# One TensorE operation instead of two for each second-layer step of a fused attention and feed-forward kernel

## The chip, the cores and the metric

The kernel runs on one core of a Trainium2 chip. The metric is the device time in microseconds of one execution: three runs of the kernel before gave 417.93, 418.27 and 418.51, the median is 418.27 us. One further execution was taken with the hardware profiler; all rows of the trace come from that one.

Engines are named as the profile names them: PE is TensorE's matmul, PEld its load of the stationary operand, DVE is VectorE, ACT is ScalarE, POOL is GpSimd and SP is SyncE, which issues the DMAs.

## The reference

The reference has two halves. The first is attention over 4 batches, 8 heads, 768 positions and 64 features: each position sees its neighbours within a window of 16 and one summary for each block of 32 positions (maximum of the keys, mean of the values). The second takes the heads together as a 512-wide x and applies a gated feed-forward block with a hidden width of 1024:

```python
xk = mu_k * x + (1.0 - mu_k) * x_prev
xr = mu_r * x + (1.0 - mu_r) * x_prev
k = np.maximum(xk @ w_k, 0.0)
v = k * k @ w_v
r = 1.0 / (1.0 + np.exp(-(xr @ w_r)))
return r * v
```

x_prev is x one position earlier. The change is in `k * k @ w_v`, the second layer.

## The kernel before

**How precision is kept.** Most products are made with numbers split in two: a high part in TensorE's rounded 32-bit format and a low part that holds the rest. A product a @ w is then three products that add up in one bank: high a with high w, high a with low w, low a with high w.

**The halves.** Each batch is worked in two halves of 384 positions (`hf`), three tiles of 128. For every half but the two of the last batch there is: attention for four pairs of heads; the mixing of x and x_prev and its split; the gate (`gate_tile`, lines 717 to 719, 12 products of 512 columns to a tile); and `experts` (from line 740), the two layers. The last batch has its own path (`last_batch` and `seven`, lines 893 to 1050; its products stand at lines 929 and 1020), with no second-layer step of the kind that is changed.

**The two layers.** `experts` goes through the hidden width in eight tiles j of 128. `first(j)` makes 12 products of 384 columns into one bank (line 757, "e1"), then relu (ACT, line 764) and square (ACT, line 766). The square r is split: its high part kh is a copy on DVE (line 770) or on ACT (line 771), whichever the schedule chooses, and its low part kl is r minus kh, on DVE (line 772). `second(j)` (products at line 784, "e2") adds this tile's share to three result banks `acc`, one for each tile of positions. The step is split in two operations: e2a does for each bank the products of kh with the high and low weights, six in all, and waits for kh; e2b does for each bank the product of kl with the high weights, three in all, and waits for kl. The last step, j = 7, is three operations, one to a bank, each with its two products of kh and one of kl; DVE multiplies each finished bank by the gate (line 814), and SP stores it.

In the very first half the first five tiles (`PLAIN`) use unsplit numbers ("single"): four products for e1 and three for e2, slower ones, with no kl. The order of emission is first(0), first(1), second(0), first(2), second(1), and so on.

**Banks.** PSUM has eight banks. Four, the pool `mm`, serve the two layers and the gate: during a half three hold `acc` and one is left for e1. The other four serve attention; from batch 1 on they are one pool, `at`, of which a score operation takes four and a values operation two (lines 550, 358 to 364).

**What sets the order.** No order is written by hand. Each operation is told to a planner (`Plan`, line 133) with its engine, its length in ns from the table `LENGTH` (line 40), a due time, and what it reads and writes. `schedule` (line 171) first carries due times backwards: an operation must be done in time for those that read its result. Then it plays through the whole kernel, and gives each engine in turn the ready operation that can start earliest, by due time where several can start at once (line 237). Engines work off their lists strictly in this order on the chip; waits are semaphores. A changed length, due time or dependency may therefore change the order of everything that follows in the plan, on each engine and in SP's DMA queue too. Attention for a batch (score, line 559, masks at 585, exponentials at 589, normalisation on POOL at 601, transposes on DVE at 626, values at 656) is placed by this planner among the products of the batch before it.

Of the kernel before, what the change touches and what calls it, by code (L numbers as in the profile page):

```python
# [32 lines left out]
NTT = HT // P  # L33
# [5 lines left out]

LENGTH = dict(  # L40
    score=950, values2=1715, score2=1600, transpose=350, vturn=110, vpool=800, vsel=330, spread=540, spread_p=900, values=1020, gate=2740, gate32=930, e1=2100,
    e1_32=2690, e2a=1400, e2b=705, e2=705, e2_32=2600, e2l_32=930,
    warm=223, kred=865, kred2=470, kmax=90, kcopy=280, vred=865, mask=204, rc=320, evac=470, mixd=535, sub=475, khv=280,
    result=600, wbits=340, wor=610, wsub=605, tiny=60,
    exp=380, pts=375, vm=160, mixa=515, cast=405, relu=380, square=425, sigmoid=500, sigmoid3=1600, wscale=570, wcast=530,
# [87 lines left out]
class Plan:  # L133
# [4 lines left out]
    def buf(self, pool, dtype=F32, in_turn=True):  # L138
        n = self.count[pool] if in_turn else None
        self.count[pool] += in_turn  # L140
        self.unplaced[pool] += 1
        return Buf(pool, n, dtype)

    def op(self, eng, cost, due, emit, reads=(), writes=(), size=0, other=None):

        bufs = []
        for x, _ in list(reads) + list(writes):
            if isinstance(x, Buf) and x not in bufs:
                bufs.append(x)
        ways = {eng: (LENGTH.get(cost, 0), emit)}  # L150
        if other:
            ways[other[0]] = (LENGTH[other[1]], other[2])
        o = Op(len(self.ops), ways, due, bufs, size)
        for x in reads:
            o.deps.update(self.writers.get(x, ()))
        for x in writes:
            o.deps.update(self.writers.get(x, ()))
            o.deps.update(self.readers.get(x, ()))
        for x in reads:
            self.readers.setdefault(x, []).append(o)  # L160
        for x in writes:
            self.writers[x] = [o]
            self.readers[x] = []
        o.deps.discard(o)
        for x in bufs:
            x.users.append(o)
        self.ops.append(o)
        o.name = cost
        return o
# [139 lines left out]
def tile_kernel(ctx: ExitStack, tc: tile.TileContext, q, k, vT, v, consts, w_k, w_v, w_r, out):  # L309
# [7 lines left out]
    def slots(name, n, shape):  # L317
        return [Slot(const, f"{name}{i}", shape) for i in range(n)]
# [13 lines left out]
        kh=slots("kh", 2, [P, HT]), kl=slots("kl", 2, [P, HT]),  # L332
# [37 lines left out]
    op, buf = plan.op, plan.buf  # L370
# [21 lines left out]
    def e1_due(b, hf, j):  # L392
        if b + hf == 0:
            return GATE0 + 11000 + STEP0 * j
        return gate_due(b, hf) + 8400 + STEP * j

    def e2_due(b, hf, j):
        return e1_due(b, hf, j + 1) + 2200

    w_f, w_h, w_l = {}, {}, {}  # L400
# [339 lines left out]
    def experts(b, hf, x, z):  # L740

        plain = PLAIN if b + hf == 0 else (0, 0)
        tiles_of = [(j + (max(PLAIN) if (b, hf) == (0, 1) else 0)) % NCV for j in range(NCV)]
        acc, ks = [], {}

        def first(j):
            ps, r = buf("mm"), buf("r")
            single = j < plain[0]
            kh, kl = ks[j] = (r, None) if j < plain[1] else (buf("kh", F32R), buf("kl", F32R))
            h, l = (w_f["wk", tiles_of[j]], None) if single else (w_h["wk", tiles_of[j]], w_l["wk", tiles_of[j]])  # L750
            terms = [(h, 0)] if single else [(h, -2), (h, -1), (l, -2)]

            def products():
                n = 0
                for w, s in terms:
                    for p in range(NPAIR):
                        nc.tensor.matmul(ps.t[:, 0:HT], w.t[:, p * P:(p + 1) * P], x[p][s].t,  # L757
                                         start=(n == 0), stop=(n == len(terms) * NPAIR - 1))
                        n += 1

            op("PE", "e1_32" if single else "e1", e1_due(b, hf, j), products,
               reads=list(dict.fromkeys([(pair[s], 0) for pair in x for _, s in terms] + [(w, 0) for w, _ in terms])),
               writes=[(ps, 0)])
            op("ACT", "relu", None, lambda: nc.scalar.activation(r.t, ps.t[:, 0:HT], AF.Relu),  # L764
               reads=[(ps, 0)], writes=[(r, 0)])
            op("ACT", "square", None, lambda: nc.scalar.activation(r.t, r.t, AF.Square),  # L766
               reads=[(r, 0)], writes=[(r, 0)])
            if kl is None:
                return
            op("DVE", "khv", None, lambda: nc.vector.tensor_copy(out=kh.t, in_=r.t),  # L770
               reads=[(r, 0)], writes=[(kh, 0)], other=("ACT", "cast", lambda: nc.scalar.copy(out=kh.t, in_=r.t)))  # L771
            op("DVE", "sub", None, lambda: nc.vector.tensor_tensor(  # L772
                out=kl.t, in0=r.t, in1=kh.t.bitcast(F32), op=ALU.subtract),
               reads=[(r, 0), (kh, 0)], writes=[(kl, 0)])

        def second(j):
            kh, kl = ks[j]
            single = kl is None
            due = e2_due(b, hf, j)
            w = [(w_f["wv", tiles_of[j]], 0)] if single else [(d["wv", tiles_of[j]], 0) for d in (w_h, w_l)]  # L780

            def product(t, a, w, start=False, stop=False):
                v = w["wv", tiles_of[j]].t
                nc.tensor.matmul(acc[t].t, a.t[:, t * P:(t + 1) * P], v.bitcast(F32) if single else v, start=start, stop=stop)  # L784

            if j < NCV - 1:
                def high():
                    for t in range(NTT):
                        if single:
                            product(t, kh, w_f, start=(j == 0))  # L790
                        else:
                            product(t, kh, w_h, start=(j == 0))
                            product(t, kh, w_l)

                def low():
                    for t in range(NTT):
                        product(t, kl, w_h)

                op("PE", "e2_32" if single else "e2a", due, high, reads=[(kh, 0), *w], writes=[(a, 0) for a in acc])
                if not single:  # L800
                    op("PE", "e2b", due + 1400, low, reads=[(kl, 0), *w], writes=[(a, 0) for a in acc])
                return
            for t in range(NTT):
                def last(t=t):
                    if single:
                        product(t, kh, w_f, stop=True)
                    else:
                        product(t, kh, w_h)
                        product(t, kh, w_l)
                        product(t, kl, w_h, stop=True)  # L810

                op("PE", "e2l_32" if single else "e2", due + 700 * t, last,
                   reads=[(kh, 0), *([] if single else [(kl, 0)]), *w], writes=[(acc[t], 0)])
                op("DVE", "result", due + 4000 + 700 * t, lambda t=t: nc.vector.tensor_tensor(
                    out=z[t].t, in0=acc[t].t, in1=z[t].t, op=ALU.mult),
                   reads=[(acc[t], 0), (z[t], 0)], writes=[(z[t], 0)])
                row = hf * HT + t * P
                op("SP", "store", due + 5000 + 700 * t, lambda t=t, row=row: nc.sync.dma_start(
                    out=out[b, row:row + P, :], in_=z[t].t), reads=[(z[t], 0)], size=P * 2048)

        first(0)
        for j in range(1, NCV + 1):
            if j < NCV:
                first(j)
            if j == 1:
                acc.extend(buf("mm") for _ in range(NTT))
            second(j - 1)
# [375 lines left out]
```

## Time and profile before

| | |
|---|---|
| median of three runs | 418.27 us (417.93 to 418.51) |
| profiled execution, its own time | 418.56 us |
| its span, first to last instruction | 416.5 us |
| granted TensorE clock | 1.00 |
| DMA traffic | 79.68 MB, mean 191 GB/s |

A row of a window view gives the stretch, its length, then for each engine the busy time and number of instructions. In a row of groups stands: line, engine, operation, written and read tiles, sizes and count, then busy time, mean ns of one, and the idle time before them with what ended it. In the chain of waits a row is start, duration, engine and line; in a timeline it is start, duration, engine, line, operation and tiles, and in brackets the idle time before. A matmul's row is longer than its share of TensorE, because one is drained while the next runs; the distance from one start to the next is what it costs.

### The profile page before, as it was taken

The numbers are of one execution on the slowest core, as the hardware profiler recorded it, in microseconds if no ns is written. First come the engines' busy times: TensorE is split into PE (matmuls) and PEld (weight loads), VectorE is DVE, ScalarE is ACT, GpSimd is POOL, SyncE is SP. The second block draws the span as 40 slices with busy tenths as digits, with TensorE's granted clock in tenths as the row PEclk, the third lists the DMA queues.
The fourth block names the chain that finished last, engine by engine and source line by source line (L and its number), as shares of the span: only waits on it lengthen the run. The fifth ranks groups of instructions, "written<-read, shape, count | busy, mean of one in ns | idle before, by whom it ended". The sixth has DMA issues, their size and how long they took to land.

```text
span 416.5 us, 9788 instructions
## 1 busy us (share of the span) xinstructions
PE 409.1 (98%) x3353; PEld 348.1 (84%) x3353; DVE 344.8 (83%) x1053; ACT 286.8 (69%) x815; POOL 125.9 (30%) x255
## 2 busy tenths in 40 slices
PE   8899999999999999999999999999999999999996
PEld 7654557788888888988888888988889899999996
DVE  3889999999998799889798778569386698878993
ACT  2889999899874599547674559466595675669710
POOL 0472565534660043502252000422433030104100
PEclk9999999999999999999999999999999999999999
DMA  8996679678878577777635454487855325230012
GB/s 295 407 296 216 222 257 318 235 251 235 240 210 264 173 248 196 230 267 247 215 120 159 158 183 172 133 297 200 252 150 143 103 75 146 59 113 15 0 59 94
DMA packets 48193, 79.68 MB, mean 191 GB/s; under 512 B 6736, under 2 KB 28176, under 8 KB 48144
## 3 DMA queue, kind: packets, MB, share of 16 engines
q1 hardware_dynamic: 48000, 78.78, 58.7%
q8 instruction: 26, 0.43, 0.4%
q10 hardware_dynamic: 144, 0.28, 0.3%
q14 instruction: 23, 0.19, 0.1%
HBM read 58.68 MB, written 20.07 MB: 189 GB/s over the span
## 4 chain that ended last, share of the span: by engine, by line
PE 83%; DMA 6%; DVE 5%; ACT 5%; issue 1%; SPq 1%; DVEq 0%; ACTq 0%
PE bank L784 24%; PE bank L757 23%; PE bank L929 14%; PE bank L656 5%; PE bank L1020 4%; PE bank L559 3%; PE bank L717 3%; PE bank L718 3%; PE bank L719 3%; DMA st<-in_w_r 2%; ACT y L589 2%; DMA st<-in_w_k 2%; DMA qt<-in_q 1%; DVE st L626 1%; DVE y L585 1%
## 5 line engine op out<-in xcount | busy, mean ns | idle before, releaser
L601 POOL TENSOR_SCALAR y<-y,rc 128x120 f32<-128x120 f32 x192 | 94.4, 510 | 130.5 <-DVE mn L585 49.2
L757 PE MATMUL bank<-xs,w 128*128 128x384 f32 x556 | 111.7, 349 | 0.0
L757 PEld LDWEIGHTS bank<-xs,w 128*128 128x128 f32 x556 | 98.1, 188 | 8.5 <-issue 1.0
L589 ACT ACTIVATE y<-y,mn 128x120 f32<-128x120 f32 x192 | 73.4, 384 | 15.3 <-DVE mn L585 15.1
L784 PE MATMUL bank<-w,kh 128*128 128x512 f32 x258 | 69.5, 397 | 0.4 <-DVE kh L770 0.4
L764 ACT ACTIVATE r<-bank 128x384 f32<-128x384 f32 x48 | 23.4, 488 | 51.0 <-PE bank L757 50.5
L784 PEld LDWEIGHTS bank<-w,kh 128*128 128x128 f32 x258 | 47.2, 188 | 9.4 <-DVE kh L770 0.7
L585 DVE CUSTOM_DVE_ANT_0 y<-bank,consts_sb 128x120 f32<-128x120 f32 x192 | 41.9, 273 | 0.1
L784 PE MATMUL bank<-w,kl 128*128 128x512 f32 x129 | 39.3, 397 | 0.0
L589 ACT ACTIVATION_READ_ACCUMULATOR y<-y,mn 128x1 f32 x192 | 36.2, 189 | 0.0
L656 PEld LDWEIGHTS bank<-pts,vx 120*64 120x64 f32 x768 | 24.0, 138 | 8.3 <-issue 7.1
L929 PE MATMUL bank<-xs,w 128*128 128x384 f32 x126 | 30.8, 337 | 0.0
L626 DVE STREAM_TRANSPOSE st<-y 128x384 f32<-128x384 f32 x48 | 27.1, 567 | 3.4 <-POOL y L601 2.8
L770 DVE CAST kh<-r 128x384 fp32r<-128x384 f32 x26 | 9.6, 370 | 23.0 <-ACT r L766 23.0
L784 PEld LDWEIGHTS bank<-w,kl 128*128 128x128 f32 x129 | 23.7, 188 | 5.6 <-issue 0.2
L685 POOL TENSOR_SCALAR xa<-vx,om_sb 128x384 f32<-128x384 f32 x11 | 8.7, 793 | 60.4 <-DVE xs L699 60.4
L656 PE MATMUL bank<-pts,vx 120*64 120x64 f32 x768 | 26.8, 224 | 0.0
L559 PEld LDWEIGHTS bank<-kt,qt 64*64 64x64 f32 x768 | 20.1, 133 | 7.9 <-issue 3.4
L559 PE MATMUL bank<-kt,qt 64*64 64x120 f32 x768 | 24.9, 268 | 1.7 <-DVE kt L478 1.1
L772 DVE TENSOR_TENSOR kl<-r,kh 128x384 fp32r<-128x384 f32 x43 | 24.1, 559 | 2.7 <-ACT kh L771 1.1
L766 ACT ACTIVATE r<-r 128x384 f32<-128x384 f32 x48 | 25.2, 525 | 0.7
L717 PE MATMUL bank<-w,xs 128*128 128x512 f32 x60 | 23.7, 395 | 0.0
(374 smaller groups left out, 824.2 us busy)
## 6 DMA issues: line engine op xcount, KB each, us to landing
vx<-in_v SPq DMA_DIRECT2D x32, 384.0 KB
far<-st SPq DMA_DIRECT2D x96, 96.0 KB
pts<-far SPq DMA_DIRECT2D x24, 384.0 KB
kt<-in_k SPq DMA_DIRECT2D x15, 544.0 KB
qt<-in_q SPq DMA_DIRECT2D x32, 192.0 KB
st<-in_vT SPq DMA_DIRECT2D x12, 384.0 KB
out<-z SPq DMA_DIRECT2D x18, 256.0 KB
st<-in_w_k SPq DMA_DIRECT2D x8, 512.0 KB
```

The source lines that it names most:

```text
L559: nc.tensor.matmul(cells(to[h])[cs, i, 0:NK], t.t[hs, n * QW:(n + 1) * QW], kt.t[hs, w * KB:w * KB + NK], start=True, stop=True)
L585: op("DVE", "mask", None, lambda h=h, i=i, var=var: nc.vector.tensor_tensor_reduce(out=cells(y[h])[:, i, 0:NK], in0=cells(spot[h])[:, i, 0 ...
L589: op("ACT", "exp", None, lambda h=h, i=i: nc.scalar.activation(cells(y[h])[:, i, 0:NK], cells(y[h])[:, i, 0:NK], AF.Exp, bias=mn[h].t[:, i ...
L601: op("POOL", "norm", None, lambda h=h, i=i: nc.gpsimd.tensor_scalar(out=cells(y[h])[:, i, 0:NK], in0=cells(y[h])[:, i, 0:NK], scalar1=rc.t ...
L626: op("DVE", "flip", due - (FIRST_AHEAD if b == 1 else AHEAD) + 8000 + 600 * h, lambda h=h: nc.vector.transpose(out=turned()[:, :, h], in_= ...
L656: nc.tensor.matmul(av.t[hs, w * QW:(w + 1) * QW], windows(vw)[:, w, hs], weights_of(pts)[0:NK, 2 * c:2 * c + 2, h, i], start=True, stop=True)
L717: nc.tensor.matmul(ps.t, xh.t[:, ts], h, start=(p == 0), stop=False)
L757: nc.tensor.matmul(ps.t[:, 0:HT], w.t[:, p * P:(p + 1) * P], x[p][s].t, start=(n == 0), stop=(n == len(terms) * NPAIR - 1))
L766: op("ACT", "square", None, lambda: nc.scalar.activation(r.t, r.t, AF.Square), reads=[(r, 0)], writes=[(r, 0)])
L772: op("DVE", "sub", None, lambda: nc.vector.tensor_tensor(out=kl.t, in0=r.t, in1=kh.t.bitcast(F32), op=ALU.subtract), reads=[(r, 0), (kh, 0 ...
L784: nc.tensor.matmul(acc[t].t, a.t[:, t * P:(t + 1) * P], v.bitcast(F32) if single else v, start=start, stop=stop)
L929: nc.tensor.matmul(bank.t[:, 0:HT], pair[w].t[:, col:col + P], a[k][s].t, start=(first and n == 0), stop=(n == 3 * nk - 1), skip_group_che ...
```

## The change

The operations e2a and e2b of a step with kl become one, "e2all". It reads kh and kl, so it waits for both, and has the due time of e2a. For each of the three banks in turn it issues the two products of kh and then the one of kl: nine in a row. In the planner's table the two lengths, 1400 and 705 ns, are replaced by one of 2075 ns. The unsplit steps and the last step of a half are as before.

```diff
@@ LENGTH
-    e1_32=2690, e2a=1400, e2b=705, e2=705, e2_32=2600, e2l_32=930,
+    e1_32=2690, e2all=2075, e2=705, e2_32=2600, e2l_32=930,
@@ second(j), j < NCV - 1
                         else:
                             product(t, kh, w_h, start=(j == 0))
                             product(t, kh, w_l)
-
-                def low():
-                    for t in range(NTT):
-                        product(t, kl, w_h)
-
-                op("PE", "e2_32" if single else "e2a", due, high, reads=[(kh, 0), *w], writes=[(a, 0) for a in acc])
-                if not single:
-                    op("PE", "e2b", due + 1400, low, reads=[(kl, 0), *w], writes=[(a, 0) for a in acc])
+                            product(t, kl, w_h)
+
+                op("PE", "e2_32" if single else "e2all", due, high, reads=[(kh, 0), *([] if single else [(kl, 0)]), *w],
+                   writes=[(a, 0) for a in acc])
                 return
```

## The prediction

> **What bounds the kernel now.** I first read the page: busy time by engine, then the chain that ended last.
>
> ```profile
> span 416.5 us, 9788 instructions
> ...
> PE 409.1 (98%) x3353; PEld 348.1 (84%) x3353; DVE 344.8 (83%) x1053; ACT 286.8 (69%) x815; POOL 125.9 (30%) x255
> ...
> PE 83%; DMA 6%; DVE 5%; ACT 5%; issue 1%; SPq 1%; DVEq 0%; ACTq 0%
> ```
>
> TensorE is busy 98% of the span and carries 83% of the chain. A share can mislead, so the next view cuts the span: up to where the first split second-layer step (e2 in what follows) can have an effect, the stretch with all of these steps, and the last batch, which has none.
>
> ```profile
> 72.60:106.30 33.70, 33.36 (x318) 26.96 (x316) 33.19 (x127) 31.76 (x94) 15.47 (x38) 1.00 0.78 246
> 106.30:354.20 247.90, 247.89 (x2065) 218.81 (x2066) 201.57 (x629) 161.92 (x471) 70.17 (x145) 1.00 0.61 190
> 354.20:416.50 62.30, 59.00 (x337) 58.68 (x335) 48.43 (x90) 32.73 (x71) 8.07 (x9) 1.00 0.17 56
> ```
>
> The columns are length, then busy PE, PEld, DVE, ACT, POOL, the granted clock, DMA share and GB/s. From 106.3 to 354.2 TensorE is busy 247.89 of 247.90 us at full clock: no gap is left to remove. From 72.6 to 106.3 it misses 0.34 us. The waits of TensorE say what that is:
>
> ```profile
> PE bank L559 <- DVE kt L478: 1.1, 2, 0.8
> ...
> PE bank L784 <- DVE kh L770: 0.4, 1, 0.4
> ```
>
> Only the last wait is at line 784, the second-layer products: one wait in the kernel, for a high part kh. None is for a low part kl. So the time is the sum of what TensorE issues, and the change can act in three ways: another pace of the same matmuls, a new wait, or another place for the other operations.
>
> **The change part by part.** How many steps are touched:
>
> ```profile
> L784 PE MATMUL bank<-w,kh 128*128 128x512 f32 x258 | 69.5, 397 | 0.4 <-DVE kh L770 0.4
> ...
> L784 PE MATMUL bank<-w,kl 128*128 128x512 f32 x129 | 39.3, 397 | 0.0
> ```
>
> 258 / 6 = 129 / 3 = 43 steps have a kl. Six of them are the last step (j = 7) of one of the six halves up to batch 2; the code issues those bank by bank already, one operation to a bank, and the diff leaves them alone. So 37 are merged. No matmul is removed or added, so the number of products is the same. The durations of one matmul overlap the next, so the pace is read from the chain, start to start:
>
> ```profile
> 158.33 1.39 PE bank L559 x48
> 159.72 2.28 PE bank L784 x9
> 162.00 2.11 PE bank L757 x12
> 164.11 2.08 PE bank L784 x9
> ...
> 241.65 2.04 PE bank L784 x9
> ...
> 335.51 2.10 PE bank L1020 x12
> 337.61 2.08 PE bank L784 x9
> ```
>
> An e2a and e2b that follow each other take 2.08 us for nine (231 ns each). The step at 337.61 is a last step, and its timeline is the order that the change gives to all: two kh products and one kl product, bank by bank.
>
> ```profile
> 337.45 0.63 PE L784 MATMUL bank<-w,kh 128*128 128x512 f32 x2
> 337.91 0.40 PE L784 MATMUL bank<-w,kl 128*128 128x512 f32 x1
> 338.15 0.62 PE L784 MATMUL bank<-w,kh 128*128 128x512 f32 x2
> 338.60 0.40 PE L784 MATMUL bank<-w,kl 128*128 128x512 f32 x1
> ```
>
> It takes the same 2.08 us. **Pace: 0.** The lower bound is the other bank-by-bank step, at 241.65, amid the gate's products: 2.04 us. If all 37 went over to that, the sum would change by -37 x 0.04 = -1.5 us. An upper bound comes from the same rows: nothing but an attention operation just before (2.28 against 2.08) makes nine slower, and that is counted below. I take 0, because 337.61 has the neighbours that the merged steps will mostly have (384-column products on both sides, 2.1 us), and 241.65 has not.
>
> **The boundary that goes.** Before, an attention operation could stand between e2a and e2b, as here:
>
> ```profile
> 186.36 1.62 PE L656 MATMUL bank<-pts,vx 120*64 120x64 f32 x48
> 187.91 0.96 PE L784 MATMUL bank<-w,kl 128*128 128x512 f32 x3
> ```
>
> It must now stand before or after the step. The change from one kind of product to the other costs the same wherever it is: the step after a score is 2.28 - 2.08 = 0.20 us longer, in or out of a step. A gain would need two attention operations side by side, 0.2 us for a pair. From batch 1 on a score takes all four banks of its pool (L550; the pool is filled at L363) and values takes two, so between the two kinds the masks or the evacuation must first empty them. **Place: 0**; the delay of such an operation is at most the rest of a step, 0.7 us, and TensorE has other products to fill it.
>
> **The new wait.** The merged operation waits for kl at its start; e2a waited for kh alone. Its price is how late kl is for the start of e2a. One usual step, kl on VectorE and e2a on TensorE:
>
> ```profile
> 166.20 0.55 DVE L772 TENSOR_TENSOR kl<-r,kh 128x384 fp32r<-128x384 f32 x1
> ...
> 166.03 2.27 PE L757 MATMUL bank<-xs,w 128*128 128x384 f32 x12
> 168.13 1.55 PE L784 MATMUL bank<-w,kh 128*128 128x512 f32 x6
> 169.52 0.85 PE L784 MATMUL bank<-w,kl 128*128 128x512 f32 x3
> ```
>
> kl is ready at 166.75, and e2a starts at 168.13, 1.38 us later. What hides kl is the previous step and the next first-layer product, 2.08 + 2.11 = 4.2 us between the end of e1(j) and the start of e2(j); with only the 2.11 us of e1 as cover, this kl would come 4.19 - 2.11 - 1.38 = 0.7 us late. I went through all 43 steps so. In 40 kl is ready before e2a starts; three are late. VectorE first, then TensorE:
>
> ```profile
> 105.90 0.36 DVE L770 CAST kh<-r 128x384 fp32r<-128x384 f32 x1
> ...
> 106.38 0.55 DVE L772 TENSOR_TENSOR kl<-r,kh 128x384 fp32r<-128x384 f32 x1
> ...
> 212.33 0.55 DVE L772 TENSOR_TENSOR kl<-r,kh 128x384 fp32r<-128x384 f32 x1
> ...
> 308.61 0.55 DVE L772 TENSOR_TENSOR kl<-r,kh 128x384 fp32r<-128x384 f32 x1
> ```
>
> ```profile
> 106.31 1.66 PE L784 MATMUL bank<-w,kh 128*128 128x512 f32 x6 [0.35 <-DVE kh L770]
> 107.90 1.62 PE L656 MATMUL bank<-pts,vx 120*64 120x64 f32 x48
> ...
> 212.25 1.55 PE L784 MATMUL bank<-w,kh 128*128 128x512 f32 x6
> ...
> 214.43 0.74 PE L656 MATMUL bank<-pts,vx 120*64 120x64 f32 x18
> ...
> 308.86 1.55 PE L784 MATMUL bank<-w,kh 128*128 128x512 f32 x6
> ...
> 311.03 1.62 PE L656 MATMUL bank<-pts,vx 120*64 120x64 f32 x48
> ```
>
> The kh that e2a waits for at 106.31 ends at 106.26, so a wait costs 0.05 us beyond the writer's end. With the order kept the three cost 106.93 - 106.31 + 0.05 = 0.67, 212.88 - 212.25 + 0.05 = 0.68 and 309.16 - 308.86 + 0.05 = 0.35: together 1.7 us. Behind such a wait stands the next e1 and with it the next relu, so a stall is not made good: TensorE has no other slack. But the order is not kept. The schedule picks for a free TensorE the operation that can start first, and an e2all that waits for kl is not that. At 106.31 values (L656) come next; ahead of e2all they hide its wait and also the 0.35 us now lost to kh: between -0.35 and +0.67, and I take -0.35. At 308.86 values follow at 311.03, and of 0 to +0.35 I take 0. At 212.25 the next of them is values too, at 214.43; no row here tells whether its data had landed by 212, and I take about the middle of 0 and 0.68, +0.35. The earlier due time (kl must now be ready at the step's due time, 1.4 us sooner) also puts squares, casts and subtractions ahead of attention work on ScalarE and VectorE, which speaks for less. The first e2 of a half is the tightest of the rest: its e1 is followed by only one more and a score.
>
> The step issues no DMA, and none is moved by hand; SP, POOL and the two other engines keep their work, in an order that may differ from 72.6 us on, the first relu of a step with a kl:
>
> ```profile
> 72.61 0.49 ACT L764 ACTIVATE r<-bank 128x384 f32<-128x384 f32 x1 [0.20 <-PE bank L757]
> ```
>
> **Sum**, against the profiled execution's own 418.56 us (span 416.5 and 2.06 around it): 0 (pace) + 0 (place) - 0.35 + 0.35 + 0 (waits) = 418.56. That execution lies 0.29 above the median of the runs, 418.27, so by the median **418.3 us**.
>
> **The rivals.** *kl sets the start* (slower). The merged operation turns the low part's slack into TensorE idle time: the three late steps keep their place and lose 1.7 us, 420.0 us. It decides from 0.84 us of such waits in all. For it: 33.19 of 33.70 us of VectorE are busy from 72.6 to 106.3, and kl stands behind attention and weight pieces there. Against it: 40 steps have slack, and the order can go round the rest.
>
> *The new order harms the crowded stretch* (slower). One vector operation like the reduction of the keys,
>
> ```profile
> 163.87 0.95 DVE L466 TENSOR_REDUCE kg<-kt 128x48 f32<-128x768 f32 x1
> ```
>
> ahead of a kh or kl, delays a step with nothing to fill it; two of these cost 1.9 us, 420.2 us. For it, the same 33.19 of 33.70; against it, that all eight first-layer products of the next half are there to be issued.
>
> *Nine in a row settle at the quick pace* (faster): -1.5 us, 416.8 us. For it, 2.04 at 241.65; against it, 2.08 at 337.61 in the same order, beside the neighbours that count.
>
> *One operation fewer saves its signalling* (faster). The bound by rows: nine products in two operations (164.11) and in three (337.61) take 2.08 alike, so an operation's end is worth 0 on TensorE, at most 37 x 0.04 = 1.5 us by the 2.04, and I give it a third of that, 0.5 us, 417.8 us, on its own no change that can be told. The Trainium skill, TensorE: Matmul & The Clock Gate, "The cost: per-tile semaphore tail", has each completion increment serialize at about 26.3 ns where many small tiles signal; an estimate by that figure is 37 x 26.3 ns = 1.0 us, 417.3 us. By that rule a step of three operations would be 26 ns longer than one of two; the trace has 2.08 for both and does not bear it out here.
>
> *The change does nothing that shows*, since TensorE never waited at the boundary: that is the forecast itself.
>
> **How the numbers follow.** A measurement of this kernel tells about 0.2% (0.84 us) from no change. Forecast, within 0.2%: 0.50. Late kl: 0.22. Crowded stretch: 0.07. Quick pace: 0.13. Signalling saved beyond 0.84 us: 0.04. A better order in the crowded stretch, worth more than its 0.34 us of idle: 0.04. Faster 0.13 + 0.04 + 0.04 = 0.21, same 0.50, slower 0.29. The forecast's own range is 417.5 to 419.1. The range for 8 in 10 goes up past the two slower cases, to 420.4, and down to 416.9, just short of the quick pace in full; that leaves out about 0.07 below and 0.08 above.
>
> **What would show it.** Pace: nine at line 784 at 2.08 us in the chain beside 384-column products; 2.04 there would be the quick pace. Waits: one line "L784 <- DVE kl L772" of at most some tenths in the waits of TensorE, and the 0.4 for kh gone; 1 us or more there is the first rival. Place: no score or values amid a step, and steps after one still 2.28. Crowded stretch: TensorE's idle time from 72.6 to 106.3 over 0.34 us is the second rival. The prediction is wrong if TensorE's busy time between the same points moves by more than 0.8 us with no wait named, or if the last batch starts (line 1020) more than 0.8 us from 335.5.

## The result

The changed kernel took 421.72 us (median of 7 runs, 419.73 to 421.96) against 418.51 us for the kernel before on the same chip (7 runs, 417.93 to 419.06). The ratio is 1.0058, with a 95% interval of 1.0042 to 1.0074: slower, by about 2.4 us. (The ratio is estimated from all runs and is not that of the medians, which lie 3.2 us apart: three runs of the changed kernel took 419.7 to 420.4 us and four took 421.7 to 422.0.) The prediction was no measurable change, 418.3 us with a range of 416.9 to 420.4. The profiled execution of the changed kernel is its quickest run, 419.73 us, so its profile shows less than the usual loss.

From its page, the span, the busy time and the chain by engine:

```profile
span 417.9 us, 9786 instructions
...
PE 409.5 (98%) x3353; PEld 348.5 (83%) x3353; DVE 341.4 (82%) x1053; ACT 286.4 (69%) x814; POOL 124.1 (30%) x256
...
PE 82%; ACT 6%; DMA 6%; DVE 3%; issue 1%; SPq 1%; DVEq 0%; ACTq 0%
```

TensorE does the same work (409.5 us busy, 409.1 before) in a span 1.4 us longer. The same three stretches as before, and the waits of TensorE:

```profile
72.60:106.30 33.70, 33.70 (x337) 27.28 (x337) 32.62 (x128) 31.49 (x96) 15.36 (x37) 1.00 0.75 232
106.30:354.20 247.90, 245.92 (x2042) 216.91 (x2039) 197.80 (x626) 160.94 (x468) 67.95 (x146) 1.00 0.61 190
```

```profile
PE bank L656 <- DMA pts<-far: 2.0, 2, 1.3
PE bank L440 <- POOL zero_sb L1062: 1.0, 1, 1.0
```

The stretch that had no gap now misses 1.98 us of TensorE, and a wait that the kernel before did not have accounts for it. It is not at line 784. It is at line 656, the values products of attention, which wait twice for pts, the attention weights that a DMA brings back from memory. The 0.4 us wait of line 784 for kh is gone, and no wait of a second-layer matmul for kl is named.

Where the two waits stand, in the timeline of TensorE, with the row of the chain for the transfer that ends the first:

```profile
101.37 4.35 PE L757 MATMUL bank<-xs,w 128*128 128x384 f32 x24
105.65 0.92 PE L656 MATMUL bank<-pts,vx 120*64 120x64 f32 x24
107.88 0.92 PE L656 MATMUL bank<-pts,vx 120*64 120x64 f32 x24 [1.31 <-DMA pts<-far]
108.73 0.73 PE L784 MATMUL bank<-w,kh 128*128 128x512 f32 x2
...
138.60 0.92 PE L656 MATMUL bank<-pts,vx 120*64 120x64 f32 x24 [0.67 <-DMA pts<-far]
```

```profile
101.54 6.20 DMA pts<-far
```

A values operation serves both halves of a pair of heads, 24 products with the pts of each. Before, e2a stood ahead of the first such operation (106.31), and values began at 107.90. Now values begin right behind the second e1, at 105.65. The pts of the first half is there; that of the second, issued at 101.54, lands at 107.74, and TensorE stands still in between. The kernel before got this fetch no sooner: issued at 100.89, it was complete, by its semaphore, at 107.64. What moved is the product that reads it. A values operation takes 1.55 us start to start where nothing waits. This one takes 3.08 (105.65 to 108.73) and the one at 137.02 takes 2.44 (to 139.45): 1.53 + 0.89 = 2.4 us lost. The wait for kh (0.4) is saved, so is one change between kinds of product, since e2 is no longer cut there (0.2), and the new order is 0.2 us ahead at the two e1 in front of it (101.37 for 101.61). That leaves 1.6 us; the last batch starts 1.5 us later (336.89 for 335.35), and the span is 1.4 us longer.

### The profile page after: what moved, and what is told of

Same layout as the page of the kernel before. It is cut to its first block, busy times and chain, and to the rows that moved or that the text cites. A ratio compares the mean times of both kernels' runs of the same rounds, so it can differ in the third digit from the quotient of the medians.

```text
span 417.9 us, 9786 instructions
## 1 busy us (share of the span) xinstructions
PE 409.5 (98%) x3353; PEld 348.5 (83%) x3353; DVE 341.4 (82%) x1053; ACT 286.4 (69%) x814; POOL 124.1 (30%) x256
## 4 chain that ended last, share of the span: by engine, by line
PE 82%; ACT 6%; DMA 6%; DVE 3%; issue 1%; SPq 1%; DVEq 0%; ACTq 0%
PE bank L784 24%; PE bank L757 23%; PE bank L925 14%; PE bank L656 5%; PE bank L1016 4%; PE bank L559 3%; PE bank L718 3%; PE bank L719 3%; PE bank L717 3%; DMA pts<-far 2%; ACT y L589 2%; DMA st<-in_w_r 2%; DMA qt<-in_q 1%; PE bank L608 1%; DVE xs L688 1%
## 5 line engine op out<-in xcount | busy, mean ns | idle before, releaser
L601 POOL TENSOR_SCALAR y<-y,rc 128x120 f32<-128x120 f32 x192 | 92.2, 499 | 137.5 <-DVE mn L585 49.1
L757 PE MATMUL bank<-xs,w 128*128 128x384 f32 x556 | 111.8, 349 | 0.0
L784 PE MATMUL bank<-w,kh 128*128 128x512 f32 x258 | 82.0, 398 | 0.0
L784 PE MATMUL bank<-w,kl 128*128 128x512 f32 x129 | 50.9, 395 | 0.0
L656 PEld LDWEIGHTS bank<-pts,vx 120*64 120x64 f32 x768 | 24.2, 138 | 10.2 <-issue 7.3
L925 PE MATMUL bank<-xs,w 128*128 128x384 f32 x130 | 32.6, 336 | 0.0
L656 PE MATMUL bank<-pts,vx 120*64 120x64 f32 x768 | 27.2, 225 | 2.0 <-DMA pts<-far 2.0
L466 DVE TENSOR_REDUCE kg<-kt 128x48 f32<-128x768 f32 (+1 forms) x17 | 15.3, 898 | 13.5 <-DMA kt<-in_k 13.3
L688 DVE SCALAR_TENSOR_TENSOR xa<-vx,consts_sb,xa 128x384 f32<-128x384 f32 x40 | 23.8, 621 | 0.4 <-ACT xa L682 0.4
```

What stands on the lines that cost most here:

```text
L601: op("POOL", "norm", None, lambda h=h, i=i: nc.gpsimd.tensor_scalar(out=cells(y[h])[:, i, 0:NK], in0=cells(y[h])[:, i, 0:NK], scalar1=rc.t ...
L656: nc.tensor.matmul(av.t[hs, w * QW:(w + 1) * QW], windows(vw)[:, w, hs], weights_of(pts)[0:NK, 2 * c:2 * c + 2, h, i], start=True, stop=True)
L688: op("DVE", "mixd", None, lambda: nc.vector.scalar_tensor_tensor(out=xa.f, in0=xt.t[:, 1 + lo:1 + lo + HT], scalar=mu_sb[:, which, p:p + 1 ...
L925: nc.tensor.matmul(bank.t[:, 0:HT], pair[w].t[:, col:col + P], a[k][s].t, start=(first and n == 0), stop=(n == 3 * nk - 1), skip_group_che ...
```

## The experiments

They ran at three other times, each time beside the kernel before (medians 419.03, 419.16 and 418.82 us), so ratios are compared, not times. Where this text gives the landing of a transfer that no row shows, it is the time at which the transfer's semaphore was complete in that run's trace. Three theories were put against each other. A: the new order has put values ahead of the landing of their pts. B: nine products bank by bank in one operation are themselves slower. C: the wait for kl costs.

**Nine in a row, at the place of e2b in the plan of before.**

```diff
                 def low():
                     for t in range(NTT):
+                        product(t, kh, w_h, start=(j == 0))
+                        product(t, kh, w_l)
                         product(t, kl, w_h)
...
+                def nothing():
+                    pass
...
-                op("PE", "e2_32" if single else "e2a", due, high, ...
+                op("PE", "e2_32" if single else "e2a", due, high if single else nothing, ...
```

> The plan is that of the kernel before, operation for operation; only what is issued differs: the place of e2a issues nothing, and the place of e2b issues all nine products bank by bank. No order and no due time has changed. Theory A (the new order put two values operations ahead of the landing of their weights pts): as the kernel before, 418.5 +-0.5 us, no wait of L656 for pts, nine products still 2.08 us. Theory B (nine products bank by bank in one operation are themselves slower): 420 us or more, nine products over 2.12 us. Theory C (the wait for kl costs): no wait for kl arises here either, so 418.5, and the next kernel tells it from A.

Ratio 1.0014 (0.9999 to 1.0029): the same as before within the measurement, though the expected absence of the wait was a miss. Since e2a's place is empty, values stand first here too, at 106.60, 0.95 us later than in the changed kernel:

```profile
106.60 0.92 PE L656 MATMUL bank<-pts,vx 120*64 120x64 f32 x24
108.37 0.92 PE L656 MATMUL bank<-pts,vx 120*64 120x64 f32 x24 [0.85 <-DVE sm L595]
```

The 0.85 us stand at the same product as the 1.31 of the changed kernel. The releaser named is an event that fell nearby: that product does not read sm, and the semaphore of the pts transfer is complete 0.03 us before the wait ends. All merged steps are in this kernel, so theory B is worth at most 0.3%, and the 0.85 us wait is a part of that.

**The changed kernel, with values put back behind the first merged step.**

```diff
+        first(at("e2all", 2), at("values2", 0))
+        first(at("e1", 3 + 7), at("values2", 3))
         waiting = {o: len(o.deps) for o in self.ops}
```

Here `at(name, n)` is the operation of that name with number n, counted from 0, and `first(o, then)` adds an edge of order to the plan after the due times are set.

> The changed kernel, with two extra edges of order in the plan: the first values operation of batch 1 behind the first merged step of its half, the fourth behind the e1 that follows. Theory A: the waits of L656 for pts (2.0 us in the profile of the changed kernel) fall under 0.3 us; in their place the first merged step of the half waits for kl, by 0.7 to 1.2 us; time 419.0 to 419.8 us, and the runs lie within 1 us of each other (the changed kernel's spread over 2.2). Theory B (the products): 421 us or more, unchanged. Theory C (kl): the same 1 us of wait for kl at the first step, and more of it in the later steps, over 2 us in all.

Ratio 1.0006 (0.9985 to 1.0026): the loss is gone. Of its waits, TensorE has none for pts. (One run of 12 was at 422.33, the others between 418.69 and 420.22, so the spread was not as small as expected.) The step at 106.8, first VectorE's rows, then TensorE's; lines stand 9 further down in this kernel:

```profile
106.37 0.35 DVE L779 CAST kh<-r 128x384 fp32r<-128x384 f32 x1
106.84 0.55 DVE L781 TENSOR_TENSOR kl<-r,kh 128x384 fp32r<-128x384 f32 x1
```

```profile
106.77 0.73 PE L793 MATMUL bank<-w,kh 128*128 128x512 f32 x2 [0.30 <-DVE kh L779]
107.44 0.50 PE L793 MATMUL bank<-w,kl 128*128 128x512 f32 x1
...
109.26 1.62 PE L665 MATMUL bank<-pts,vx 120*64 120x64 f32 x48
```

The merged operation starts at 106.77, and kl is written until 106.84 + 0.55 = 107.39. So the operation does not wait for kl at its start: its first two products go ahead on kh alone, and the third, at 107.44, is the one that needs kl. The expected wait of 0.7 to 1.2 us was a miss; it is the same 0.3 us for kh as in the kernel before.

**The kernel before, with values put ahead.** The same two edges the other way round: values before e2a, and values before e1.

> The kernel before, split in e2a and e2b as it was, with two extra edges of order in the plan: the first values operation of batch 1 ahead of the first e2a of its half, the fourth ahead of the e1 that it followed. Theory A: without any merged step the wait of L656 for pts appears, 1.5 to 4 us, and the time is 420 to 422.5 us with a spread of over 1 us. Theories B and C (products, kl): nothing of the change is in it, 418.5 +-0.5 us.

Ratio 1.0041 (1.0022 to 1.0060), with no merged step in it. In the profiled execution, the quickest of the 12 runs, the first values operation had its data almost in time (1.78 us to the next step, 106.12 to 107.90, for the usual 1.55); the fourth waited, by less than the 1.5 us that were expected:

```profile
136.20 0.92 PE L665 MATMUL bank<-pts,vx 120*64 120x64 f32 x24
138.34 0.92 PE L665 MATMUL bank<-pts,vx 120*64 120x64 f32 x24 [1.21 <-DMA pts<-far]
```

**The changed kernel once more.** No edit.

> The changed kernel again, to see whether its runs of about 420 and about 421.8 us differ by the wait for pts. Theory A: time of the profiled execution minus the wait of L656 for pts is 417.7 +-0.4 us whichever kind is profiled (419.73 - 2.0 in the first profile). Theory B or C: the wait stays near 2.0 us and another row of TensorE grows.

Ratio 1.0062 (1.0033 to 1.0091). The execution that was profiled this time is one of the longer ones, 422.68 us, and shows one way to lose more. First the timeline, then a window with the granted clock in the third column from the end:

```profile
106.08 0.92 PE L656 MATMUL bank<-pts,vx 120*64 120x64 f32 x24
109.73 1.55 PE L656 MATMUL bank<-pts,vx 120*64 120x64 f32 x24 [2.74 <-DVE wc L844]
111.21 1.22 PE L784 MATMUL bank<-w,kh 128*128 128x512 f32 x2
112.23 0.63 PE L784 MATMUL bank<-w,kl 128*128 128x512 f32 x1
112.66 0.88 PE L784 MATMUL bank<-w,kh 128*128 128x512 f32 x2
```

```profile
110.00:113.00 3.00, 3.00 (x28) 2.58 (x26) 2.92 (x9) 1.52 (x6) 2.92 (x7) 0.50 0.46 117
```

The same product waits 2.74 us instead of 1.31 (by its semaphore, the transfer issued at 102.09 landed at 109.60; what is named is again a neighbour). Of the 16 updates of that semaphore 15 were in by 107.97, and the last came 1.63 us later. And behind so long a pause TensorE is granted 0.50 of its clock: one product takes 112.66 - 112.23 = 0.43 us where 0.23 is usual. The Trainium skill, TensorE: Matmul & The Clock Gate, Part 1, says that an idle array falls to half its clock and earns it back by activity; the 0.43 us agree with half the clock. The Trainium skill puts the idle time that does it at a window of about 3.4 us there, and here 2.74 us was enough. My sum (time less the wait is 417.7) was a miss: 422.68 - 2.74 = 419.9, since the clock and a later start of values (106.08) come on top. The second place has no wait in this execution, and one merged step further on waits 0.2 us for kl.

**Only the fourth values operation put back.** The second of the two edges alone.

> The changed kernel with one extra edge of order: only the fourth values operation of batch 1 goes back behind the e1 that follows; the first stays ahead of the merged step. Theory A (wait for pts at two places, the first being the larger): the first wait stays (1.5 to 3.6 us, values at about 106), the second (0.9 us) is gone; 419.8 to 422.5 us, above the kernel of e2_values_behind. Theory C (kl at the start of the merged step): the values operation of the first place hides kl, so 418.5 us.

Ratio 1.0036 (1.0020 to 1.0052). One wait for pts is left, in the place of the first:

```profile
PE bank L664 <- DMA pts<-far: 1.3, 1, 1.3
```

The wait is a little under the 1.5 us that were expected. So the first place alone makes the kernel slower; what the merged step gains from the cover, the 0.3 us wait for kh that it has with values put back, is less than that.

**The need for kl alone, products as before.**

```diff
-                op("PE", "e2_32" if single else "e2a", due, high, reads=[(kh, 0), *w], ...
+                op("PE", "e2_32" if single else "e2a", due, high, reads=[(kh, 0), *([] if single else [(kl, 0)]), *w], ...
```

> The kernel before, e2a and e2b split, products in their old order, lengths 1400 and 705; the plan alone is told that e2a too needs kl. Theory A: the added need by itself is enough, the plan puts the first values operation ahead of e2a and TensorE waits for pts there, 1 to 3.6 us; 419.8 to 422.5 us. Theory B (nine products in one operation): 418.5 +-0.5 us of the kernel before.

Ratio 1.0063 (1.0042 to 1.0084), the whole loss, with e2a and e2b apart and their products in the old order:

```profile
107.30 0.92 PE L656 MATMUL bank<-pts,vx 120*64 120x64 f32 x24
109.75 0.92 PE L656 MATMUL bank<-pts,vx 120*64 120x64 f32 x24 [1.53 <-DVE mn L585]
110.60 1.66 PE L784 MATMUL bank<-w,kh 128*128 128x512 f32 x6
```

Values again stand ahead of e2a and wait at their second half; the row names a neighbour, and the fetch landed at 109.66. It is not the whole of the loss here. The new order also makes score products wait for the masks from 97 to 100 us, which they do not in the changed kernel:

```profile
PE bank L559 <- DVE mn L585: 1.1, 3, 0.7
```

This settles it against theory B: what costs is what the planner is told, not what TensorE is given.

**The old length in the plan.** `e2all=2105` for 2075.

> The changed kernel with 2105 ns, the sum of the two old lengths, in place of 2075 in the plan. Theory A: the plan still puts the first values operation ahead of the merged step with no margin to the landing it expects; the wait is there, 420 to 422.7 us as the changed kernel. Rival (the shorter length of the plan made the order): 418.5 to 419.5 us.

Ratio 1.0062 (1.0042 to 1.0082), as the changed kernel; the length did not make the order.

```profile
PE bank L656 <- DMA pts<-far: 2.1, 2, 1.3
```

**What else is on the DMA engines.** Two kernels clear SP's queue around the issue of the second pts. In the first, the three stores of results there (256 KB each) may not start before 106 us of the plan; in the second, neither they nor the two loads of values inputs (384 KB each) may start before 108 us. The code of the second:

```diff
+        for n in range(3):
+            at("store", n).after = 108000
+        for o in self.ops:
+            if o.n in (1022, 1023):
+                o.after = 108000
```

> The changed kernel; in the plan the three stores of the first half's results, 256 KB each, which stand on SP's queue around the fetch of the second pts, may not start before 106 us of the plan. The values operation stays ahead of the merged step. Theory A with the crowded DMA engines as cause of the late landing: issue to landing of the second pts falls from 6.2 us to under 5.5, the wait of values falls under 0.8 us and the time under 420 us. Theory A with the landing late for another reason (its 4 KB rows, the puts before it): the wait stays at 1.5 us or more, because the plan also moves the values operation forward with the landing that it expects.

> The changed kernel; beside the three stores of e6 the two loads of the next values inputs (384 KB each) that SP issues around the second pts may not start before 108 us of the plan either. The values operation stays ahead of the merged step. If the DMA engines, 1.01 busy while the second pts is under way in the changed kernel (101.5 to 107.8 us, 341 GB/s), are what makes it land late: issue to landing under 5 us, wait of values for it under 0.8 us, 418.7 to 420.3 us. If not: the wait stays at 1.5 us or more, and the time at 421 us or more.

With the stores alone moved: ratio 1.0059 (1.0036 to 1.0081), and no help, which is what was expected if crowded DMA engines are not the reason. The plan expects the transfer sooner and moves loads up; on the chip the wait was longer, and the transfer landed at 109.02, 7.85 us after its issue (lines stand 9 further down; the row named again has only an event nearby). A pts row is 3 KB (384 KB over 128 partitions), not 4 KB.

```profile
101.17 0.33 SPq L648 DMA_DIRECT2D pts<-far  x1
...
109.15 0.92 PE L665 MATMUL bank<-pts,vx 120*64 120x64 f32 x24 [1.89 <-DVE vx L680]
```

With the loads out of the way too, values still stand first, and do not wait:

```profile
99.78 1.40 SPq L651 DMA_DIRECT2D pts<-far  x2
...
106.47 1.62 PE L668 MATMUL bank<-pts,vx 120*64 120x64 f32 x48
108.02 0.73 PE L796 MATMUL bank<-w,kh 128*128 128x512 f32 x2
```

The windows while the second pts is under way, in the changed kernel, the kernel with the stores alone moved, and this one; the last two columns are the DMA engines' busy share and GB/s:

```profile
101.50:107.80 6.30, 5.07 (x49) 4.68 (x47) 6.23 (x38) 6.27 (x21) 2.67 (x8) 1.00 1.01 341
```

```profile
101.20:109.10 7.90, 6.07 (x53) 5.51 (x51) 7.83 (x41) 7.86 (x24) 3.64 (x11) 1.00 0.89 254
```

```profile
100.84:105.34 4.50, 4.50 (x25) 4.24 (x24) 4.47 (x22) 4.44 (x8) 3.24 (x10) 1.00 0.96 273
```

Here the second fetch was issued at 100.84 and complete at 105.34, 4.5 us later, at a DMA share of 0.96; in the changed kernel it took 6.2 us at 1.01, and with the stores alone moved 7.85 us at 0.89. So the share does not order the times. What is least in this kernel is the amount that was moved meanwhile: an estimate from these rows is 273 x 4.5 = 1.2 MB, against 341 x 6.3 = 2.1 and 254 x 7.9 = 2.0 MB. That fits a fetch that shares the engines with what is queued beside it, but no run shows what made the 7.85 us. The ratio is 1.0029 (1.0012 to 1.0045), better than the changed kernel's and still not level. Two waits of TensorE are in this kernel and not in the changed one:

```profile
PE bank L571 <- DMA qt<-in_q: 1.2, 1, 1.2
...
PE bank L796 <- DVE kl L784: 0.6, 1, 0.6
```

The first stands at 6.57 us, long before the change or the held loads can act. The other stands at 257.76, where a product of a merged step waits for its kl: there the new wait does cost something. What else keeps this kernel from level is not shown.

None of these kernels is quicker than the kernel before; the best with merged steps equals it.

## Why the prediction was wrong

**Pace: right.** Nine products, bank by bank in one operation, take what e2a and e2b took. The chain of the changed kernel:

```profile
163.59 2.11 PE bank L757 x12
165.70 2.08 PE bank L784 x9
...
169.89 2.15 PE bank L784 x9
...
243.22 2.04 PE bank L784 x9
```

2.08 us beside first-layer products and 2.04 amid the gate's, as read before; the 2.15 is explained below. Neither the quick pace nor a saving by fewer completions came: the step of one operation takes what steps of two and three did. The 26.3 ns for each completion that the Trainium skill gives for many small tiles (TensorE: Matmul & The Clock Gate, "The cost: per-tile semaphore tail") do not show.

**Place: right for the change of kinds.** A step behind a score still takes 2.28 us:

```profile
159.92 1.39 PE bank L559 x48
161.31 2.28 PE bank L784 x9
```

**The new wait: its premise was wrong.** I wrote that the merged operation waits for kl at its start. The step at 106.77 with values put back shows that it waits at its third product, 0.46 us later at the usual pace. The changed kernel itself has such a step, VectorE's row first:

```profile
169.55 0.55 DVE L772 TENSOR_TENSOR kl<-r,kh 128x384 fp32r<-128x384 f32 x1
```

```profile
169.73 0.63 PE L784 MATMUL bank<-w,kh 128*128 128x512 f32 x2
170.19 0.46 PE L784 MATMUL bank<-w,kl 128*128 128x512 f32 x1
```

kl is written until 170.10, 0.37 us into the step, and the step takes 2.15 us instead of 2.08. By that, the three late steps would have cost 0.2, 0.2 and nothing, not 0.67, 0.68 and 0.35. But the planner knows an operation only as a whole: it is told that all of it needs kl, and holds it back for that. So kl itself cost next to nothing on the chip (0.07 us in this profile; one wait of 0.2 to 0.6 us in each of four other profiled executions with merged steps) and yet changed the order, as it did where e2a alone was told of it.

**The step that failed** is the term of -0.35 us: "At 106.31 values (L656) come next; ahead of e2all they hide its wait". Values did come ahead, as foreseen. I had priced this place from kl alone, "between -0.35 and +0.67". For 212.25 I had asked whether the data of values had landed, but not here, where values were to start 2.25 us sooner, at 105.65 for 107.90. It measured +1.53 us start to start in one execution and 3.58 in another (5.13 from the start of values to the next step, less 1.55, part of it at half the clock); the wait for kh was saved as foreseen. In the plan that the kernel makes, values start at the very moment at which the transfer is expected, 105.85 us on the plan's clock, and the chip had it at 107.74; the plan of the kernel before had expected it at 105.36 and put values 1.18 us behind that, and e2a's own wait on the chip added to the margin. The bound should have come from the row for SP's issue of that pts and from the DMA share of this window, both in the kernel before:

```profile
100.89 0.44 SPq L639 DMA_DIRECT2D pts<-far  x1
```

```profile
100.90:107.90 7.00, 6.65 (x35) 5.64 (x33) 6.85 (x39) 6.96 (x20) 2.60 (x9) 1.00 1.04 337
```

There the fetch took 6.75 us and landed at 107.64. Values put behind the second e1 could start at 105.96 (106.31 - 0.35), and their second half 0.78 us later, at 106.74: by these numbers a wait of about 0.9 us, where I had written a gain.

**The terms for 212.25 and 308.86** (+0.35 and 0) measured 0: there the order stayed, and no wait stands at either step in the changed kernel. At the first of them kl now came earlier, at 213.78 for a start at 213.85.

**Not foreseen:** the second place, 0.89 us, where a values operation went ahead of an e1, far from any late kl. There too the plan leaves no margin: it starts values at 135.54 and expects their fetch at 135.47, where the plan before had 137.11 and 136.21. In the experiment that put it back alone the first place remained; the second place alone was not tried.

**The rivals.** The slower ones named a late kl and the crowded VectorE; both had the sign, and neither the mechanism. The sign that I had set for the second, TensorE idle for over 0.34 us from 72.6 to 106.3, is absent: it is busy 33.70 of 33.70 us. The crowded engines of that stretch were the DMA engines, before as after. My test for a wrong prediction was met: the last batch starts 1.5 us later, over the 0.8 us that I had allowed.

**What stays open.** Two executions of the changed kernel were profiled, and why most runs take about 421.8 us is not shown. The half clock is not the reason for all of them: the mean granted clock of each run is on record, and it is 0.996 in the runs of 421.72 and 421.96 us (0.995 in the profiled one of 422.68), but 1.000 and 0.999 in those of 421.81 and 421.82. That these two had a longer wait is argued only. What makes one fetch take 6.2 us and another 7.5 in the same kernel is open too, and of the transfers around it, loads without stores were not tried.

## What to carry to other kernels

Where a list schedule feeds engines that work in order, an added dependency is priced by what the planner will put in its place, and that operation's own data must be followed to their landing, not to their issue. Here a wait belonged to the instruction that reads the operand, not to the group that the planner knows; a planner that is told of the group pays for waits that the chip does not have. An operation that other work was covering, here values behind e2a, has a price as soon as the cover is moved.

## What the runs showed that was not expected

One fetch of 384 KB took from 4.5 to 7.85 us from issue to landing in the same stretch of different kernels, and 6.2 and 7.5 us in two executions of one kernel, at DMA shares between 0.89 and 1.04 that do not follow the times. In the kernel before it landed at 107.64 for a second half of values at 108.68 (107.90 + 0.78): it had 1 us to spare, and nothing in the waits showed it. And a pause of 2.74 us, not of 1.3 or 1.9, cost the following products half their clock, about 0.9 us more (the first merged step took 3.1 us instead of 2.2).
